# An adaLN transformer block on one core: weight loads, LN and modulation work reordered at the start, output transposes in two banks, and other slot counts

## Chip, cores and metric

The kernel runs on one core of a Trainium2 chip. Times are device microseconds of one execution; medians are over several executions. The profile is of one execution. A single-core program has no second die to compare with, so a run counts as slow only when it lies over 1.5% above the fastest of the same kernel.

## The reference

One block: a conditioning vector `c` gives six modulation vectors; then modulated layer norm (LN), attention over the last 512 cached keys and values (32 query heads, 4 KV heads), a gated residual, a second modulated LN, a SwiGLU FFN, and a gated residual.

```python
mod = (silu(c) @ w_mod).reshape(1, 6, 1, 1024)          # c: (1, 1024), w_mod: (1024, 6144)
sa, ca, ga, sb, cb, gb = (mod[:, i] for i in range(6))
h = layernorm(x) * (1 + ca) + sa                         # x: (1, 2048, 1024)
q = h @ wq                                               # 32 heads of 128
o = softmax(q @ k[-512:].T * 128**-0.5) @ v[-512:]       # per head; 8 query heads share a KV head
x = x + ga * (o @ wo)
h = layernorm(x) * (1 + cb) + sb
x = x + gb * ((silu(h @ w_gate) * (h @ w_up)) @ w_down)  # F = 3584
```

All inputs are bf16. The inputs, weights and matmuls are the same before and after.

## The kernel before

The tokens are processed in four chunks of 512. Everything is held transposed (features on partitions): `xT`, `hT`. A small recording layer (`T.op`) emits each instruction on its engine with the semaphore waits that its reads and writes of named buffers need. **Each engine, and the queue that issues the DMAs (SP), runs what it was given in program order** (moving one GpSimd instruction moved the squares behind it from 46.23 to 9.30 us, below), so where an operation stands in the program is a decision about what it waits behind.

The prologue, in program order (cuts marked with `...`):

```python
for t in range(4):                       # x tiles of chunk 0
    load_x_tile(t); transpose_x_tile(t)
for gi in range(4):                      # first third of w_mod, 3 slots of 1 MB
    load_wm(gi); mod_mm(gi)
mod_readout(0, 2 * DT, ...)              # shift and scale for the first LN
for t in range(4, 16):                   # the other x tiles, through 4 buffers
    load_x_tile(t); transpose_x_tile(t)
arena.reset()                            # K, V, wq slots overlap the w_mod slots
...
for gk in range(Hkv): T.op(Q_k, ... load K head gk ..., writes=[B_knat])   # one buffer record, one semaphore
for gk in range(Hkv): T.op(Q_v, ... load V head gk ..., writes=[B_vaug])
T.op(POOL, lambda: g.memset(v_aug[:, :, P:VW], 1.0), writes=[B_vaug])      # ones column of V
load_wq(0, 0); load_wq(0, 1)
... transpose K on TensorE ...
drain(ln1_task(0, OPB))                  # LN of chunk 0, whole: squares on POOL, sums on PE, ...
for ch in range(1, NCH): add_ln("ln1", ch, ln1_task(ch, OPB))   # background, a step at a time
```

All four K loads write one buffer record on one semaphore, so each waits for the landing of the one before it; the same for V. The memset waits for all V loads, and the LN's squares come after the memset on GpSimd (POOL).

The attention loop is software-pipelined: iteration `i` runs the query projection of head `i`, scores of `i-1`, PV of `i-2`, the output transpose of `i-3`, and one background step. In chunk 0 it also carries the rest of the modulation, 32 pieces:

```python
if i < 32:  load_wm_late(16 + i)                      # 128 columns of w_mod: rows of 256 bytes
if 2 <= i < 34:
    mod_mm_late(16 + i - 2)                           # 8 matmuls of one column into bank OA
...
qproj(i)                                              # 8 matmuls 128x512 into bank QB
if 0 <= i - 1 < NA: scores(i - 1)
if 0 <= i - 2 < NA: pv(i - 2)                         # into OA and OBT; VectorE scales out of OA (L573)
if 0 <= i - 3 < NA: otr(i - 3); ...
run_bg(1)
```

The modulation pieces share PSUM bank `OA` with PV. They stand first in an iteration, so they wait until VectorE has scaled the previous PV result out of that bank.

At the end of each FFN chunk the result is transposed back, all four tiles through one bank:

```python
for tt in range(TPC):
    for dt in range(DT): transpose(bb[...], xT[:, dt, ...], ..., PB[YTB])   # bank 6 every time
    T.op(DVE, lambda: V.tensor_copy(xnat[sl][:, :], bb[:, 0:D]), writes=[PB[YTB], B_xnat[sl]])
    T.op(Q_out[sl], ... store ...)
```

The softmax here doesn't subtract the row's maximum and nothing guards it: scores larger than these inputs give would overflow.

## Time and profile before

| | before |
|---|---|
| median of 16 runs | 1476.13 us (1475.0 to 1482.43) |
| span of the profiled run | 1473.2 us |
| TensorE busy / VectorE / ScalarE / GpSimd | 93% / 40% / 31% / 5% |
| first query projection ends | 70.25 us |

From the page of the kernel before: span, and two of the rows in 40 slices (busy tenths of TensorE, and granted TensorE clock in tenths of full speed).

```profile
span 1473.2 us, 20801 instructions
...
PE   4488889999999999999999999999999999989997
...
PEclk7599999999999999999999999999999999999999
```

TensorE is busy 90% or more in all slices but two from the seventh on (220 us), so time can mainly be won where it is not: at the start, and in gaps too short for such a row to show. The prologue, in the timeline of all engines (start us, duration us, engine, line, operation, out<-in, shapes, count, and in brackets the idle time before it and what ended it):

```profile
38.20 1.89 PE L288 MATMUL ps<-ident,arena 128*128 128x128 bf16 x16 [6.51 <-DMA arena<-in_A_k_cache_dram]
...
46.14 0.13 POOL L498 MEMSET arena<- 128x32 bf16 x1 [44.49 <-DMA arena<-in_A_v_cache_dram]
46.23 17.00 POOL L402 TENSOR_TENSOR ln_sq<-xT 128x512 bf16<-128x512 bf16 x16
...
54.31 0.61 PE L284 MATMUL ps<-ln_sq,ones_bf 128*128 128x512 bf16 x1 [0.39 <-POOL ln_sq L402]
55.03 0.69 DVE L415 SCALAR_TENSOR_TENSOR ln_var<-ps,ln_msq 128x512 f32<-128x512 f32 x1 [10.70 <-PE ps L284]
...
63.99 5.59 ACT L440 ACTIVATE hT<-ln_n,c6a,g 128x512 bf16<-128x512 bf16 x7 [0.82 <-DVE ln_n L437]
...
69.64 0.61 PE L284 MATMUL ps<-hT,arena 128*128 128x512 bf16 x1 [0.19 <-ACT hT L440]
```

The second line is the telling one: GpSimd had been idle for 44.49 us waiting for V, for a memset of 0.13 us, while x of chunk 0 had been in place since 9 us. The squares behind it, the variance behind them and the whole LN chain follow from there.

TensorE's timeline in chunk 0, and below the dots in chunk 1, where no modulation is left:

```profile
85.93 0.34 PE L284 MATMUL ps<-sc_bf,xnat 128*128 128x1 bf16 x8 [0.77 <-DVE arena L573]
86.13 1.89 PE L284 MATMUL ps<-hT,arena 128*128 128x512 bf16 x8
...
90.81 0.34 PE L284 MATMUL ps<-sc_bf,xnat 128*128 128x1 bf16 x8 [0.77 <-DVE arena L573]
...
330.39 1.89 PE L284 MATMUL ps<-hT,arena 128*128 128x512 bf16 x8
...
334.14 1.89 PE L284 MATMUL ps<-hT,arena 128*128 128x512 bf16 x8
```

An iteration takes 4.88 us (90.81 - 85.93) in chunk 0 and 3.75 us (334.14 - 330.39) in chunk 1. Of the 1.13 us between them, 0.20 us are the eight small matmuls themselves (86.13 - 85.93); 0.93 us is the wait, of which the profile names 0.77 us.

The output transposes of the second of the four chunks of the FFN, in TensorE's timeline:

```profile
1153.34 0.50 PE L288 MATMUL ps<-ident,xT 128*128 128x128 bf16 x6
...
1155.81 0.62 PE L288 MATMUL ps<-ident,xT 128*128 128x128 bf16 x8 [0.79 <-DVE xnat L729]
...
1158.62 1.04 PE L288 MATMUL ps<-ident,xT 128*128 128x128 bf16 x8 [0.79 <-DVE xnat L729]
1159.45 5.80 PE L284 MATMUL ps<-hT,arena 128*128 128x512 bf16 x21
```

Each tile waits 0.79 us for the copy out of the single bank. The trace's clock record has half clock granted from 1158.3 us for 3.4 us. Two groups from the list by form (busy us, mean ns, then idle before them and its releasers) sum the waits up:

```profile
L288 PE MATMUL ps<-ident,xT 128*128 128x128 bf16 x128 | 12.1, 232 | 12.3 <-DVE xnat L729 9.4 <-DVE xT L717 2.9
...
L284 PE MATMUL ps<-sc_bf,xnat 128*128 128x1 bf16 x256 | 10.9, 163 | 22.9 <-DVE arena L573 22.9
```

### The profile page before, as it was taken

To read this page: it belongs to the slowest core of one execution; us is meant where nothing else is said; L and a number is where in the kernel's file an instruction comes from. 1 tells how busy PE (TensorE), PEld (TensorE's weight loads), DVE (VectorE), ACT (ScalarE), POOL (GpSimd) and SP (SyncE) were. 2 spreads that over 40 slices of the span, in tenths; PEclk is the share of its full clock that TensorE was granted. 3 is DMA by queue.
4 is the path that set the end of the run, shared out by engine and by line. 5 is a ranking of instruction groups with operands and counts; after the bars stand their busy time and mean duration, and the time that the engine had idled before them with its cause. 6 is when DMAs were issued, how large, how long until landed. Compare 5 with 4: busy or idle time off the path is not lost.

```text
span 1473.2 us, 20801 instructions
## 1 busy us (share of the span) xinstructions
PE 1369.9 (93%) x8592; PEld 704.7 (48%) x8592; DVE 595.5 (40%) x1268; ACT 453.3 (31%) x722; POOL 68.7 (5%) x73
## 2 busy tenths in 40 slices
PE   4488889999999999999999999999999999989997
PEld 3144554456554556545564444444444444444443
DVE  3344554366561456515563144313431233123411
ACT  0255554266560466505673013201110011001100
POOL 0402001210001000010000100000000000000000
PEclk7599999999999999999999999999999999999999
DMA  7365440452214612046111774235633375328112
GB/s 239 103 165 137 108 108 30 115 161 74 74 39 114 172 58 87 30 114 172 59 58 31 227 228 144 100 101 193 222 115 100 123 234 171 94 92 270 59 51 79
DMA packets 262319, 178.55 MB, mean 121 GB/s; under 512 B 41040, under 2 KB 258128, under 8 KB 262224
## 3 DMA queue, kind: packets, MB, share of 16 engines
q1 hardware_dynamic: 262224, 177.22, 40.3%
q8 instruction: 67, 1.10, 0.3%
q14 instruction: 28, 0.23, 0.0%
HBM read 173.02 MB, written 4.19 MB: 120 GB/s over the span
## 4 chain that ended last, share of the span: by engine, by line
PE 89%; DVE 4%; DMA 2%; ACT 2%; issue 2%; POOL 0%; SPq 0%; DVEq 0%; ACTq 0%
PE ps L284 86%; PE ps L288 2%; DVE arena L573 1%; DMA arena<-in_w_mod_dram 1%; ACT arena L550 1%; DVE xT L717 1%; DMA arena<-in_A_v_cache_dram 1%; DVE xnat L729 1%; DMA arena<-in_A_k_cache_dram 1%; ACT hT L440 1%; POOL ln_sq L402 0%; DVE rl L570 0%; ACT L550 0%; ACT L422 0%; DMA xnat<-in_A_x_dram 0%
## 5 line engine op out<-in xcount | busy, mean ns | idle before, releaser
L284 PE MATMUL ps<-arena 128*128 128x512 bf16 (+1 forms) x4480 | 675.5, 307 | 14.8 <-DVE xT L717 11.0
L284 PE MATMUL ps<-hT,arena 128*128 128x512 bf16 x2816 | 635.9, 381 | 17.2 <-ACT hT L440 11.7
L284 PEld LDWEIGHTS ps<-arena 128*128 128x128 bf16 x4480 | 366.8, 98 | 339.2 <-issue 17.5
L284 PEld LDWEIGHTS ps<-hT,arena 128*128 128x128 bf16 x2816 | 269.4, 98 | 328.6 <-issue 11.9
L550 ACT ACTIVATE arena<-ps 128x512 bf16<-128x512 f32 x512 | 305.8, 597 | 295.0 <-PE ps L284 259.3
L697 ACT ACTIVATE arena<-ps 128x512 bf16<-128x512 f32 x112 | 66.9, 597 | 528.5 <-PE ps L284 528.5
L698 DVE SCALAR_TENSOR_TENSOR arena<-arena,ps 128x512 bf16<-128x512 bf16 x112 | 77.1, 688 | 175.9 <-ACT arena L697 175.9
L538 DVE CAST arena<-ps 128x512 bf16<-128x512 f32 x128 | 88.5, 691 | 85.1 <-PE ps L284 82.0
L402 POOL TENSOR_TENSOR ln_sq<-xT 128x512 bf16<-128x512 bf16 x64 | 67.8, 1081 | 734.7 <-PE ps L284 711.8
L701 DVE SCALAR_TENSOR_TENSOR arena<-arena,ps 128x512 bf16<-128x512 bf16 x112 | 77.1, 688 | 53.6 <-PE ps L284 53.5
L717 DVE SCALAR_TENSOR_TENSOR xT<-ps,c,xT 128x512 bf16<-128x512 f32 x32 | 22.6, 746 | 184.8 <-PE ps L284 184.8
L598 DVE SCALAR_TENSOR_TENSOR xT<-ps,c,xT 128x512 bf16<-128x512 f32 x32 | 24.0, 750 | 164.1 <-PE ps L284 164.1
L573 DVE TENSOR_TENSOR arena<-ps,rl 128x384 bf16<-128x384 f32 x128 | 71.4, 558 | 4.5 <-DVE rl L570 0.2
L569 DVE RECIPROCAL rl<-ps 128x3 f32<-128x3 f32 x128 | 23.1, 180 | 113.3 <-PE ps L284 113.3
L288 PE MATMUL ps<-ident,arena 128*128 128x128 bf16 x528 | 51.1, 221 | 7.9 <-DMA arena<-in_A_k_cache_dram 6.5
L584 DVE COPY arena<-ps 128x512 bf16<-128x512 bf16 x128 | 53.1, 415 | 0.2 <-PE ps L288 0.2
L575 DVE TENSOR_SCALAR arena<-ps,rl 128x128 bf16<-128x128 f32 x128 | 45.0, 351 | 4.6
L288 PEld LDWEIGHTS ps<-ident,arena 128*128 128x128 bf16 x528 | 35.6, 98 | 8.3 <-DMA arena<-in_A_k_cache_dram 6.7
L440 ACT ACTIVATE hT<-ln_n,c,g 128x512 bf16<-128x512 bf16 x32 | 25.8, 809 | 28.3 <-DVE ln_n L437 28.2
L440 ACT ACTIVATE hT<-ln_n,c6a,g 128x512 bf16<-128x512 bf16 x32 | 25.7, 811 | 23.2 <-DVE ln_n L437 23.2
L284 PE MATMUL ps<-sc_bf,xnat 128*128 128x1 bf16 x256 | 10.9, 163 | 22.9 <-DVE arena L573 22.9
L437 DVE TENSOR_TENSOR ln_n<-ln_t,ln_B 128x512 bf16<-128x512 bf16 x64 | 30.0, 469 | 1.3 <-DVE ln_t L434 0.2
(46 smaller groups left out, 246.1 us busy)
## 6 DMA issues: line engine op xcount, KB each, us to landing
arena<-in_A_wq_dram SPq DMA_DIRECT2D x32, 1024.0 KB, 5.4
arena<-in_A_wo_dram SPq DMA_DIRECT2D x16, 2048.0 KB, 9.8
arena<-in_B_w_gate_dram SPq DMA_DIRECT2D x28, 1024.0 KB, 5.2
arena<-in_B_w_up_dram SPq DMA_DIRECT2D x28, 1024.0 KB, 7.0
arena<-in_B_w_down_dram SPq DMA_DIRECT2D x16, 1792.0 KB, 10.1
xnat<-in_w_mod_dram SPq DMA_DIRECT2D x32, 256.0 KB, 3.1
xnat<-in_A_x_dram SPq DMA_DIRECT2D x16, 256.0 KB, 3.6
arena<-in_w_mod_dram SPq DMA_DIRECT2D x4, 1024.0 KB, 8.2
```

The lines of the kernel that those rows point to most:

```text
L284: T.op(PE, lambda: TE.matmul(out_ap, lhsT, rhs, start=start, stop=stop), reads=reads, writes=[bank_buf])
L288: T.op(PE, lambda: TE.transpose(out_ap, in_ap, ident[:, :]), reads=reads + [B_ident], writes=[bank_buf])
L402: T.op(POOL, lambda: g.tensor_tensor(ln_sq[dt][:, :], xT[:, dt, chs], xT[:, dt, chs], ALU.mult), reads=[B_xT[dt][ch]], writes=[B_sq[dt]])
L440: T.op(ACT, lambda: A.activation(hT[:, dt, chs], ln_n[sl][:, :], AF.Identity, bias=ccol[:, shift_base + dt:shift_base + dt + 1], scale=gco ...
L538: T.op(DVE, lambda: V.tensor_copy(qT_s[qs], bank(QB)), writes=[PB[QB], B_qT[qs]])
L550: T.op(ACT, lambda: A.activation(ex_s[es][:, kt, :], bank(b), AF.Exp, scale=att_scale), writes=[PB[b], B_ex[es]])
L573: T.op(DVE, lambda: V.tensor_tensor(o_s[os_][:, 0:3, :], in3, rl3, ALU.mult), reads=[B_rl], writes=[PB[OA], B_os[os_]])
L575: T.op(DVE, lambda: V.tensor_scalar(o_s[os_][:, 3, :], bank(OBT, P, 0), rl[:, 3:4], None, op0=ALU.mult), reads=[B_rl], writes=[PB[OBT], B_ ...
L584: T.op(DVE, lambda: V.tensor_copy(oT_all[:, h, :], bb[:, 0:CH]), writes=[PB[TRB], B_oT[h]])
L697: T.op(ACT, lambda: A.activation(th_s[ts_], bank(gb), AF.Tanh, scale=0.5), writes=[PB[gb], B_th[ts_]])
L698: T.op(DVE, lambda: V.scalar_tensor_tensor(out=t1_s[ts_], in0=th_s[ts_], scalar=1.0, in1=bank(gb), op0=ALU.add, op1=ALU.mult), reads=[B_th ...
L701: T.op(DVE, lambda: V.scalar_tensor_tensor(out=guT[:, ft, :], in0=t1_s[ts_], scalar=0.5, in1=bank(ub), op0=ALU.mult, op1=ALU.mult), reads= ...
```

## The change

Its intent: start the attention loop early, keep TensorE from waiting in chunk 0 and at the output, and give the FFN weights other slot counts. The core of the diff (renamings, asserts and the general sizing of the slots left out):

```diff
-            NWM = 3
+            NWM = 4
+            arena.off = ARENA_BYTES - NWM * DT * 512 * 2      # w_mod slots lie over oT_all, not over K, V, wq
...
+            ln0 = ln1_task(0, OPB, "act")                      # squares of chunk 0 on ScalarE
+            for _ in range(DT + 7):                            # statistics of LN 0 before the modulation
+                next(ln0)
             for gi in range(G1_READY + 1):
                 load_wm(gi)
                 mod_mm(gi)
             mod_readout(0, 2 * DT, c6a, B_c6a, 0, g1, B_g1, DT)
-            for t in range(TPC, ST):
-                load_x_tile(t)
-                transpose_x_tile(t)
...
-            Q_k = dq("q_k"); Q_v = dq("q_v")
+            Q_k = [dq("q_k%d" % i) for i in range(Hkv)]; Q_v = [dq("q_v%d" % i) for i in range(Hkv)]
...          # B_knat, B_vaug: one record per head as well
             load_wq(0, 0)
-            load_wq(0, 1)
+            drain(ln0)                                         # normalise, scale and shift: 8 activations
...
-            drain(ln1_task(0, OPB))
+            for t in range(TPC, 2 * TPC):
+                load_x_tile(t)
+            load_wq(0, 1)
...          # in the loop, i < 32:
-                    if i < NJ - JT0:
-                        load_wm_late(JT0 + i)
-                    if 2 <= i < NJ - JT0 + 2:
-                        mod_mm_late(JT0 + i - 2)
+                    if i == LATE_STEP * k: load_wm_late(gi)                  # 8 loads of 1 MB into unused hT, every 4th
+                    if TPC <= i < len(XT_REST): load_x_tile(XT_REST[i])
+                    if 1 <= i <= len(XT_REST): transpose_x_tile(XT_REST[i - 1])   # 12 x tiles, one each
                     qproj(i)
+                    if i == LATE_STEP * k + LATE_LEAD: mod_mm_late(gi)       # 32 matmuls, AFTER qproj
...
-                run_bg(1)
+                run_bg(2 if <an LN1 task is queued> else 1)
...          # last LN step of every chunk but the first: ScalarE activation -> VectorE tensor_scalar
...          # FFN
-            NWG = 3; NWD = 2
+            NWG = 2; NWD = 3
...
+                    yb = [6, 7][t % 2]                         # output transposes alternate banks
+                    bb = bank_bf(yb)
```

## The prediction

> **What bounds the kernel now.** From about 75 us on, TensorE. The timeline shows attention repeating every 3.75 us with no TensorE gap (chunk 1), FFN groups equally gapless, and matmuls 0.216 us apart. The chain of waits puts 89% on TensorE. That core of work is untouched. The time that can be won lies elsewhere:
>
> 1. *Prologue.* The first query projection ends at 70.2 us. Timeline: x tiles until 31 us, K loads one after another until 38 us, V loads until 46 us, and only then (GpSimd runs them behind the memset that waits for V) eight squares of 1.0 us until 54 us; then variance, Ln, a 1.28 us table load, Exp, and eight 0.81 us ScalarE activations.
> 2. *Late modulation in chunk 0.* Iterations take 4.88 us, not 3.75: 8 one-column matmuls (0.20 us) wait 0.77 us for VectorE's scaling that frees their bank. The group of sc_bf,xnat matmuls shows 22.9 us idle in front.
> 3. *Output transposes.* Per chunk three waits of 0.79 us for the copy out of the single bank: 9.4 us in all.
>
> **Prologue after.** The four w_mod loads, K, V and wq no longer wait for arena slots. LN of chunk 0 is taken before the modulation, squares on ScalarE. Estimate from the durations above: x transposed at 9 us, squares (0.8 us each, like the other bf16 activations) until 15.6, variance 17, Ln/table/Exp/B until 21; modulation matmuls 17 to 21, readout 22, then 8 x 0.81 us: first projection over near 30 us. Gain 40 us. The first matmuls stay slow: the Trainium skill (TensorE: Matmul & The Clock Gate, Part 1) says an idle array runs at half clock until about 3.4 us of activity; here spacing is 0.43 us until 75.7 us, then 0.21, and the granted clock between 40 and 80 us was 0.59.
>
> **Chunk 0 after.** 32 x 1.13 us goes. Back come 8 batches of 32 one-column matmuls (0.8 us each, 6.4 us; placed after the projection, when their bank has long been read); 12 x-tile transposes (8 x 0.057 us each, 5.5 us); some 4.5 us of stalls, since their copy (0.69 us) and twice the LN steps per iteration stand in VectorE's queue ahead of the score banks' release, and Ln, Exp and two table loads now meet in one iteration. Net gain 20 us.
>
> **FFN.** Two output banks: about 7.5 us of the 9.4. Gate/up double-buffered instead of triple: a 2 MB load lands in 7 us, needed after 13.8; with the 1.8 MB down-weights about 13 us of DMA per 13.8 us group: just enough, no gain. Activation moved to VectorE (0.3 to 0.7 us each, estimate): VectorE 40% busy, off the path; ScalarE's relief worth 1 us at most.
>
> Sum: 40 + 20 + 7.5 + 1 = 69: **1407 us, range 1394 to 1422**. Faster by over 2%: 0.97; within 2%: 0.03; slower: 0.00.
>
> **What would show it.** First query projection ending at 28 to 33 us; chunk 0 from there to its last output transpose about 151 us (171 before); no TensorE wait for the scaling before sc_bf matmuls; waits for the output copy under 2 us in all; chunks 1 to 3 and the gate/up stretches unchanged in length, no TensorE wait on gate or up weights.
>
> **What would make it wrong.** The weight loads sharing bandwidth so that the fourth w_mod or wq lands after 30 us; score banks stalling over 1 us in each of 12 iterations; gate/up weights late with two slots (several us per chunk); granted clock falling as density rises.

## The result, and the profile after

| | before | after |
|---|---|---|
| median | 1476.13 us (16 runs) | 1402.97 us (8 runs, 1400.38 to 1403.41) |
| ratio of fast runs | | 0.9495 (0.9483 to 0.9507) |
| span of the profiled run | 1473.2 us | 1399.8 us |
| mean granted clock | 0.979 | 0.995 |

Ratios here and below are the mean time of one kernel's fast runs over that of the other's of the same rounds, so not quite the ratio of the medians quoted.

The predicted 1407 us, range 1394 to 1422, held. Where the 73.4 us between the two profiled runs lie is read by cutting both at the same points of the program: the end of the first query projection, the first and the last read-out of attention's output projection, and the end. The busy time of each engine in each of these stretches, before and then after (start:end and length; busy us and instructions of TensorE, its weight loads, VectorE, ScalarE, GpSimd; granted clock, DMA share, GB/s):

```profile
0.00:70.25 70.25, 31.00 (x296) 18.46 (x296) 25.43 (x45) 11.81 (x14) 17.97 (x25) 0.68 0.59 180
70.25:249.10 178.85, 151.05 (x1369) 90.05 (x1370) 85.70 (x224) 92.20 (x149) 8.21 (x8) 0.98 0.43 113
249.10:846.80 597.70, 587.77 (x4097) 324.21 (x4096) 287.23 (x706) 272.59 (x435) 41.52 (x39) 1.00 0.35 98
846.80:1473.20 626.40, 600.08 (x2832) 272.00 (x2830) 197.09 (x294) 76.71 (x124) 1.04 (x1) 0.99 0.44 140
```

```profile
0.00:30.20 30.20, 16.66 (x202) 10.75 (x203) 14.37 (x33) 16.06 (x22) 1.02 (x9) 0.81 0.95 304
30.20:192.10 161.90, 154.25 (x1482) 95.96 (x1480) 100.77 (x252) 90.24 (x145) 24.45 (x24) 0.99 0.48 146
192.10:784.10 592.00, 582.78 (x4082) 322.21 (x4081) 295.58 (x738) 238.24 (x391) 32.91 (x31) 1.00 0.34 97
784.10:1399.80 615.70, 597.38 (x2832) 270.79 (x2830) 199.18 (x302) 70.70 (x116) 1.04 (x1) 1.00 0.45 144
```

Prologue 40.05 us less, chunk 0 16.95, the rest of attention 5.7, the FFN 10.7: together 73.4. The busy time of TensorE in the FFN barely moves; the length does.

The prologue after, in the timeline of all engines:

```profile
9.42 4.27 ACT L424 ACTIVATE ln_sq<-xT 128x512 bf16<-128x512 bf16 x8 [5.34 <-DVE xT L355]
...
15.13 2.54 PE L285 MATMUL ps<-sc_bf,arena 128*128 128x1 bf16 x96 [0.95 <-DVE ln_var L440]
...
20.57 0.51 SPq L539 DMA_DIRECT2D arena<-in_A_wq_dram  x1
...
21.38 6.38 ACT L466 ACTIVATE hT<-ln_n,c6a,g 128x512 bf16<-128x512 bf16 x8 [3.24 <-DVE ln_n L462]
...
26.61 3.59 PE L285 MATMUL ps<-hT,arena 128*128 128x512 bf16 x8 [5.27 <-DMA arena<-in_A_wq_dram]
```

The squares start at 9.42 us, as soon as x is there, and take 0.53 us each. The first projection is released by the landing of wq at 26.6 us; the last of the eight activations ends at 27.76 us (21.38 + 6.38). Two chains of nearly equal length meet here. In chunk 0 and at the output, from TensorE's timelines:

```profile
101.13 0.94 PE L285 MATMUL ps<-sc_bf,hT 128*128 128x1 bf16 x32
101.93 1.96 PE L285 MATMUL ps<-arena 128*128 128x512 bf16 x20
...
103.95 1.89 PE L285 MATMUL ps<-hT,arena 128*128 128x512 bf16 x8
...
107.70 1.89 PE L285 MATMUL ps<-hT,arena 128*128 128x512 bf16 x8
```

```profile
1088.42 0.50 PE L289 MATMUL ps<-ident,xT 128*128 128x128 bf16 x6
...
1090.88 1.22 PE L289 MATMUL ps<-ident,xT 128*128 128x128 bf16 x16 [0.34 <-DVE xnat L792]
1091.94 3.40 PE L285 MATMUL ps<-hT,arena 128*128 128x512 bf16 x15
```

The 32 modulation matmuls take 0.80 us with no wait, and an iteration without them takes 3.75 us already in chunk 0. The output transposes take 3.52 us (1091.94 - 1088.42) at full clock; before it was 6.11 us in the chunk shown and 5.74 us in the chunk ahead of it. The groups that answer to the two of before:

```profile
L289 PE MATMUL ps<-ident,xT 128*128 128x128 bf16 x128 | 10.5, 220 | 4.3 <-DVE xT L779 2.9 <-DVE xnat L792 1.4
...
L285 PE MATMUL ps<-sc_bf,hT 128*128 128x1 bf16 x256 | 7.5, 163 | 0.0
```

### The profile page after: what moved, and what is told of

Same layout as the page of the kernel before. It is cut to its first block, busy times and chain, and to the rows that moved or that the text cites. A ratio compares the mean times of both kernels' runs of the same rounds, so it can differ in the third digit from the quotient of the medians.

```text
span 1399.8 us, 20688 instructions
## 1 busy us (share of the span) xinstructions
PE 1351.1 (97%) x8592; PEld 699.7 (50%) x8592; DVE 609.9 (44%) x1324; ACT 415.2 (30%) x674; POOL 59.4 (4%) x65
## 4 chain that ended last, share of the span: by engine, by line
PE 93%; DVE 2%; ACT 2%; SPq 1%; issue 1%; DMA 0%; DVEq 0%; ACTq 0%
PE ps L285 90%; PE ps L289 3%; ACT arena L605 1%; DVE xT L779 1%; SPq L526 0%; SPq L361 0%; DMA arena<-in_A_wq_dram 0%; ACT L605 0%; ACT L447 0%; DVE xnat L792 0%; DVE arena L628 0%; SPq L530 0%; DVE ln_var L440 0%; ACT ln_var L447 0%; DVE arena L630 0%
## 5 line engine op out<-in xcount | busy, mean ns | idle before, releaser
L427 POOL TENSOR_TENSOR ln_sq<-xT 128x512 bf16<-128x512 bf16 x56 | 58.4, 1061 | 704.5 <-PE ps L285 681.1
L459 DVE TENSOR_TENSOR ln_t<-xT,ln_A 128x512 bf16<-128x512 bf16 x64 | 27.5, 430 | 0.0
L625 DVE RECIPROCAL rl<-ps 128x1 f32<-128x1 f32 x128 | 21.5, 168 | 13.6 <-PE ps L289 0.5
L285 PE MATMUL ps<-ln_sq,ones_bf 128*128 128x512 bf16 x64 | 15.1, 379 | 3.9 <-DVE arena L639 3.0
```

Of the source, the lines that this page charges most:

```text
L285: T.op(PE, lambda: TE.matmul(out_ap, lhsT, rhs, start=start, stop=stop), reads=reads, writes=[bank_buf])
L427: T.op(POOL, lambda: g.tensor_tensor(ln_sq[dt][:, :], xT[:, dt, chs], xT[:, dt, chs], ALU.mult), reads=[B_xT[dt][ch]], writes=[B_sq[dt]])
```

## The experiments

Twelve kernels. All outputs are right. The names beginning with b_ are the kernel before with one edit; those with a_ the changed kernel with one edit. They ran in three sessions, each beside its own runs of the kernel before (medians 1476.64, 1478.44 and 1476.17 us). To set an a_ kernel against the changed kernel, the text takes the difference of its ratio from 0.9495, times 1476 us; because the sessions differ, such a figure is good to about 3 us (each ratio's 95% interval is 2 to 4 us wide on either side). The trace gives the place.

| kernel | median us | ratio | against its parent | expected |
|---|---|---|---|---|
| b_mod_after_proj | 1451.63 | 0.9826 | -25.7 | -30 |
| b_two_out_banks | 1463.63 | 0.9909 | -13.4 | -8 to -10 |
| b_memset_later | 1472.44 | 0.9958 | -6.2 | -9 to -10 |
| a_mod_before_proj | 1407.12 | 0.9524 | +4.3 | +7 |
| a_one_out_bank | 1415.86 | 0.9578 | +12.3 | +9, or +11 to +17 |
| a_ln0_after_mod | 1411.94 | 0.9547 | +7.7 | +5 to +6 |
| a_wm_low | 1403.71 | 0.9494 | 0 | +5 to +8 |
| a_three_gate_slots | 1402.96 | 0.9484 | -1.6 | 0 |
| a_kv_one_by_one | 1412.44 | 0.9562 | +9.9 | +13 |
| a_x_before_loop | 1408.95 | 0.9540 | +6.6 | +2 to +5 |
| a_ln_on_scalar | 1404.45 | 0.9504 | +1.3 | 0 |
| a_four_banks_wq_first | 1386.14 | 0.9385 | -16.2 | -12 to -13 |

(The fourth column is the ratio's distance from 1, or from 0.9495, times 1476 us.)

### Chunk 0: position or batching?

The change both batches the late modulation (8 times 32 matmuls, from 1 MB loads, instead of 32 times 8 from loads of 256-byte rows) and moves it behind the projection. Two runs separate these.

```diff
 # b_mod_after_proj: kernel before
-                    if 2 <= i < NJ - JT0 + 2: mod_mm_late(...); ...
                     if h == 0: ensure_ln("ln1", ch)
                     qproj(i)
+                    if 2 <= i < NJ - JT0 + 2: mod_mm_late(...); ...
```

> Kernel before, with the 8 late modulation matmuls of each iteration emitted after the query projection instead of ahead of it; same 32 small loads of 256-byte rows, same 32 batches. Theory A (the wait for the bank on TensorE's path is the cost): iterations of chunk 0 fall from 4.88 us to 3.95 us, the 22.9 us of idle before the sc_bf,xnat matmuls fall below 2 us, and the time falls by about 30 us, to 1446 us (2.0% faster). Rival B (the many small loads or the number of batches are the cost, so that fewer and larger batches were needed): under 8 us, above 1468 us.

```diff
 # a_mod_before_proj: changed kernel
+                    for k, gi in ...: if i == LATE_STEP * k + LATE_LEAD: mod_mm_late(gi); ...
                     qproj(i)
-                    for k, gi in ...: if i == LATE_STEP * k + LATE_LEAD: mod_mm_late(gi); ...
```

> Changed kernel, with its 8 late modulation batches of 32 matmuls put back ahead of the query projection. Theory A (each batch ahead of the projection pays one bank wait of about 0.8 to 0.95 us, whatever its size): 8 x 0.9 = 7 us more than the changed kernel, 1410 us. Rival B (batching removed the cost, position does not matter): within 2 us of the changed kernel's 1403.

The kernel before with the move alone: iterations of 3.95 us (one small batch at 85.41 us, the next at 89.36), idle before the small matmuls 0.0 us instead of 22.9, and 25.7 us faster, with all 32 small loads and batches as they were. Theory A is borne out; the rival is not. Why less than 30? In the profiled runs chunk 0 became 24.5 us shorter: the wait had occurred 29 times, not 32 (29 x 0.93 = 27 us); the LN of chunk 1, at one step per shorter iteration, made TensorE wait 1.1 us more at the start of chunk 1; and half clock was granted there for 3.4 us (about 1.7 us). The rest of attention won 1.7 us and the FFN lost 4.3, in which there was more half clock; the next section has this.

The changed kernel with the batch put back ahead shows the same wait, once per batch, whatever the batch's size (0.77 us in five of the eight batches, 0.33 to 0.55 us in the three that fell among the x tiles). From TensorE's timeline of that kernel, where the same line was without a bracket in the changed one:

```profile
101.14 0.94 PE L285 MATMUL ps<-sc_bf,hT 128*128 128x1 bf16 x32 [0.77 <-DVE arena L628]
```

It cost 5.5 us between the profiled runs and 4.3 us timed, with 5.1 us of listed waits; 7 us was expected at 0.9 us for all eight. So position carries the gain. What batching adds is only that there would be 8 such waits instead of 32 if the position were bad.

### The output: waits, and something that follows them

```diff
 # b_two_out_banks: kernel before
-                bb = bank_bf(YTB)
+                    yb = [6, 7][t % 2]; bb = bank_bf(yb)       # per tile
```

> Kernel before, with the output transposes alternating between two PSUM banks, nothing else. Theory A (12 waits of 0.79 us for the copy, plus the last stretch of the kernel): 8 to 9 us less, 1467 to 1468 us. Theory B (the same, and a shorter gap also spares the half-clock stretch of 3.4 us seen at 1158 us, worth 1.7 us): about 10 us less, 1466 us, and no half clock in the FFN stretch. If the waits were not on the path: under 2 us less.

```diff
 # a_one_out_bank: changed kernel
-                    yb = [6, 7][t % 2]
+                    yb = 6
```

> Changed kernel, with the output transposes of all tiles back in one PSUM bank. Theory A (waits only): 12 waits of 0.79 us return less the 0.34 us waits of now, and the end of the kernel grows by 2 us: about 9 us more, 1412 us. Theory B (waits, and each longer stretch of transposes and waits, 5.7 us instead of 3.5 us without an ordinary matmul, is followed in some chunks by a stretch of granted half clock of 3.4 or 6.8 us, worth 1.7 or 3.4 us, where it falls being chance): 9 us and 2 to 8 us on top, 1414 to 1420 us, with half-clock records right at the output transposes; the unchanged gate/up matmuls after them run at half pace meanwhile.

Two banks alone took 13.4 us off the kernel before, and its FFN stretch became 615.9 us long, that of the changed kernel (615.7). One bank put back cost the changed kernel 12.3 us, and its FFN stretch became 627.9 us. Both are more than the waits: from 5.74 to 3.52 us is 2.2 us in each of three chunks, and the end of the kernel is 2.6 us shorter (from the first transpose that waits to the end, 8.55 and 5.99 us), 9.2 us in all. The rest follows theory B. The clock records of the profiled runs say where half clock was granted at the output transposes of the first three chunks:

| profiled run | banks | half clock at the three outputs (us granted) |
|---|---|---|
| before | 1 | 0, 3.4, 0 |
| b_mod_after_proj | 1 | 3.4, 3.4, 6.8 |
| b_memset_later | 1 | 3.4, 6.8, 6.8 |
| a_one_out_bank | 1 | 3.4, 0, 3.4 |
| b_two_out_banks, after, and 7 other a_ kernels with two banks | 2 | none, in 27 outputs |

9 of 12 outputs with one bank, none of 27 with two. The slow run, at a granted clock of 0.75 throughout, is left out. Half clock for 3.4 us costs a busy TensorE about 1.7 us, so by this estimate between 1.7 us (before) and 8.5 us (b_memset_later, 17 us of half clock) per run. Runs of the kernel before scatter accordingly: of two in one session, one took 1475.44 us at a mean granted clock of 0.979, the other 1481.08 us at 0.972 (over all 28 runs listed beside the experiments, time and clock correlate at -0.86).

The Trainium skill (TensorE: Matmul & The Clock Gate, Part 1) describes a free-running activity window of 3413 ns after which an idle array drops to half clock; the records agree: all but those that the end of the trace cuts last 3.413 us or a multiple, and in each fast trace every change of the clock lies on one grid of 3.413 us, to within 3 ns. Its Part 4 says that transposes do not count as busy in the same way. An estimate from that page's window: a stretch of 5.74 us without an ordinary matmul holds one whole window in about two of three cases ((5.74 - 3.41) / 3.41 = 0.68), one of 3.52 us in about 3%. The counts, 9 of 12 and 0 of 27, fit that, but the grid does not bear it out. In six of the 27 outputs with two banks a window covered 29 or 30 of the 32 transposes, with ordinary matmuls (all that are no transposes) busy in at most 6% of it, and full clock followed each time. So transposes in place of ordinary matmuls are not enough.

What differs with one bank is how long TensorE waits. Below is its busy time in four such windows (start:end and length; busy us and instructions; granted clock, DMA share, GB/s). The first three are of the kernel before: where the attention pipeline drains (half clock followed), the first output (full clock followed) and the second (half clock followed). The last is an output of the changed kernel (full clock followed):

```profile
786.22:789.63 3.41, 1.55 (x24) 1.00 0.00 0
1001.26:1004.67 3.41, 1.81 (x25) 1.00 0.40 154
1154.86:1158.27 3.41, 1.40 (x17) 1.00 0.26 102
...
1240.73:1244.14 3.41, 2.35 (x32) 1.00 0.03 13
```

With the grid laid over all 13 fast traces, 5036 windows after 90 us began at full clock. Where TensorE was busy for under 45% of one, half clock followed in 15 of 15; from 45% to 54.5%, in 11 of 19; above that, in none of 5002. This holds for the outputs (41% to 54% in the nine that were followed by half clock; 52% to 54% in the emptiest window of each of the other three with one bank; 69% in those six with two banks) and for the attention drain, which was followed by half clock in 7 of the 13 traces although ordinary matmuls stood less than 3.4 us apart there. So the waits thin out a window, and where the grid falls decides whether one window is thin enough. The two runs on the banks change only these waits; the rule itself is read off the traces, whose matmul ends are modelled, and no run tests its threshold.

### The prologue, piece by piece

```diff
 # b_memset_later: kernel before
-            T.op(POOL, lambda: g.memset(v_aug[:, :, P:VW], 1.0), writes=[B_vaug])
 ...
             drain(ln1_task(0, OPB))
+            T.op(POOL, lambda: g.memset(v_aug[:, :, P:VW], 1.0), writes=[B_vaug])
```

> Kernel before, with one GpSimd instruction (the memset of V's ones column) emitted after the squares of chunk 0 instead of ahead of them. Theory A (the squares stood behind a memset that waits for the last V load, though they need nothing of it): squares start at 9 us, the variance follows the K transposes at once, first query projection ends near 60 us instead of 70.2, time 9 to 10 us less, 1466 us. Rival B (the chain is set by the K and V loads themselves or by the order of TensorE's work): under 3 us less.

GpSimd's timeline of that kernel; the first line was at 46.23 us before:

```profile
9.30 8.02 POOL L402 TENSOR_TENSOR ln_sq<-xT 128x512 bf16<-128x512 bf16 x8 [7.65 <-DVE xT L351]
46.09 0.13 POOL L525 MEMSET arena<- 128x32 bf16 x1 [28.77 <-DMA arena<-in_A_v_cache_dram]
```

The first projection ended at 62.3 us instead of 70.25, so a 0.13 us memset on the wrong side of eight squares cost 8.0 us. Of that, the profiled run kept only 2.3 us in its span: its FFN stretch was 632.2 us instead of 626.4, with 17 us of half clock at the outputs. Here a gain at the start was given back by chance at the end. That is probably why only 6.2 us were timed, with runs from 1467.3 to 1473.7; the other runs have no trace.

```diff
 # a_kv_one_by_one: changed kernel
-            Q_k = [dq("q_k%d" % i) for i in range(Hkv)]; Q_v = ...
+            Q_k = [dq("q_k")] * Hkv; Q_v = [dq("q_v")] * Hkv       # and one buffer record for each
```

> Changed kernel, with one semaphore and one buffer record for all four K loads and one for all four V loads again, so each load waits for the landing of the one before. Theory A (this was the largest single piece of the prologue: in the kernel before, eight such loads took 15.5 us, 31.5 to 46 us with gaps, and wq stands behind them in the queue): K done near 28 us, V near 37, wq lands near 41, first projection ends near 44 us instead of 30.2, about 13 us more than the changed kernel, 1416 us. Rival (the place of the squares and the LN order made the gain): under 4 us more.

The K issues occupied the queue for 15.1 us and the V issues for 7.6 us; wq was issued at 33.0 us instead of 20.6, landed near 39.3, and the first projection ended at 42.9 us instead of 30.2. This is the largest single piece of the prologue that was found.

```diff
 # a_ln0_after_mod: changed kernel
-            for _ in range(DT + 7):
-                next(ln0)
```

> Changed kernel, with all of chunk 0's LN emitted after the modulation matmuls instead of its statistics ahead of them. My theory of the prologue as the trace now shows it (first projection bound by the landing of wq at 26.6 us, the LN chain only just behind with its last activation at 27.8 us): the squares still run at 9 us, but TensorE's sums wait for the fourth w_mod load, variance near 24 us, first activation near 29, first projection ends near 36 us instead of 30.2: 5 to 6 us more, 1409 us. Rival (LN chain has slack, the loads alone set the start): under 1.5 us more.

The first projection ended at 39.4 us, 9.2 later (7.7 us timed). The mechanism is the expected one, the size was not: TensorE was at half clock when it came to the first eight sums, 0.43 us each, so the variance came at 27.0 us and not 24, and the first activation at 32.4 us and not 29. The order matters although the squares still ran at 9 us.

```diff
 # a_wm_low: changed kernel
-            arena.off = ARENA_BYTES - NWM * DT * 512 * 2
```

> Changed kernel, with the four early w_mod slots at the start of the arena again, over the later K, V and wq slots. If the place in the arena matters: the first K load waits for the modulation matmuls of its slot, and wq for those of the last slot (near 19.5 us), so K lands after 22, wq after 32 us, the first projection ends at 35 to 38 us: 5 to 8 us more, 1408 to 1411 us. If not (the loads queue behind w_mod anyway): under 2 us more.

A miss: no loss in the timed runs, 2.7 us in the first projection's end (32.9 us), of which part is scatter: kernels untouched at this point ended it between 30.2 and 32.1 us. The K loads were indeed issued at 17.9 us instead of 10.2. But in the changed kernel the four K issues, begun at 10.23 us, hold the queue until 17.3 us; they stand behind 4 MB of w_mod in any case, the last of which landed at 18.5 us. The new place in the arena is worth little.

```diff
 # a_x_before_loop: changed kernel
-            XT_REST = list(range(TPC, ST))                     # one tile per iteration
+            for t in range(TPC, ST):                           # all ahead of the loop
+                if t >= 2 * TPC: load_x_tile(t)
+                transpose_x_tile(t)
+            XT_REST = []
```

> Changed kernel, with the other 12 x tiles loaded and transposed ahead of the loop (after the first LN and the K transposes) instead of one per iteration. Expected: first projection ends 9 to 12 us later (39 to 42 us); chunk 0 shorter by 12 x 0.46 us of transposes plus 1 to 3 us of stalls, 6 to 8 us; net 2 to 5 us more than the changed kernel, 1405 to 1408 us. If the in-loop copies and bank waits cost more than the model says (over 0.8 us an iteration), it is even or faster.

6.6 us slower, a little more than expected. Its profiled run was the one slow run (1796.68 us at a granted clock of 0.75); the other four lay between 1407.76 and 1411.16 us. Since only the slow run has a trace, the split between prologue and chunk 0 stays open. (Its first projection ended at 42.6 us, near the 39 to 42 expected, but at a granted clock of 0.5 to 0.75, so this is no more than a hint.)

### The parts that were predicted to do nothing

```diff
 # a_three_gate_slots: changed kernel
-            NWG = 2; NWD = 3        # and the loads one group ahead
+            NWG = 3; NWD = 2        # and the loads two groups ahead, as before
```

> Changed kernel, with three slots each for gate and up weights and two for down weights, and their load order, as before. Prediction's theory (both arrangements land in time, no TensorE wait on weights in either): within 1 us of 1403, no wait on gate, up or down loads. Rival (the new slots give part of the FFN gain of 10.7 us): 2 us or more slower.

```diff
 # a_ln_on_scalar: changed kernel
-                    if sq_eng == "act":
+                    if True:            # last LN step on ScalarE for every chunk
```

> Changed kernel, with the last LN step of every chunk on ScalarE again (0.81 us each there), all else as changed. Prediction's theory (neither engine bounds anything there): within 1.5 us of 1403. Rival (ScalarE's exps are delayed and TensorE waits for score banks): 2 us or more slower, with more TensorE idle put down to ScalarE.

Neither moved the time clear of the scatter (-1.6 and +1.3 us, with 3 us of uncertainty, and a 3.4 us half-clock stretch at the attention drain in each profiled run that the changed kernel's did not have). The traces are sharper: the FFN stretch took 615.7 us in both, as in the changed kernel, and TensorE waited for no gate, up or down weights in the changed kernel or in a_three_gate_slots. The LN step takes 0.81 us on ScalarE and 0.41 us on VectorE; nobody waits for it.

### Beyond both kernels

In the changed kernel, the largest wait of TensorE left is the same kind once more: the down projection's two accumulators, 11.0 us of listed idle. TensorE's timeline of the changed kernel:

```profile
910.33 0.38 PE L285 MATMUL ps<-arena 128*128 128x512 bf16 x1 [0.72 <-DVE xT L779]
910.90 12.04 PE L285 MATMUL ps<-arena 128*128 128x512 bf16 x55 [0.19 <-DVE xT L779]
923.66 0.38 PE L285 MATMUL ps<-arena 128*128 128x512 bf16 x1 [0.72 <-DVE xT L779]
```

```diff
 # a_four_banks_wq_first: changed kernel
-    DNB = [4, 5]
+    DNB = [[4, 5], [6, 7]]             # by pp % 2; output transposes use banks 4 and 5
 ...
+            load_wq(0, 0)              # ahead of the K and V loads instead of after them
```

> Beyond both kernels: the changed kernel with (1) the down projection's pairs of accumulators alternating between banks 4,5 and 6,7, the output transposes in 4,5, and (2) the first wq load issued ahead of K and V. From the changed kernel's waits: (1) 24 waits of TensorE on the down projection's read-out, 11.0 us, go; (2) first projection then bound by the last LN activation (27.8 us), so it ends at 28.2 to 29 us instead of 30.2, 1 to 2 us. Together 12 to 13 us, 1390 us. If bank waits of under 1 us were not wholly on the path, less than 6 us.

TensorE's timeline of that kernel, the whole down projection of a chunk:

```profile
882.70 48.51 PE L285 MATMUL ps<-arena 128*128 128x512 bf16 x220
931.05 0.50 PE L289 MATMUL ps<-ident,xT 128*128 128x128 bf16 x6
```

1386.14 us, 16.2 us less than the changed kernel and 6.2% less than before. The down projection takes 48.35 us (931.05 - 882.70) instead of 52.09 (884.02 to 936.11 in the changed kernel): 1.25 us per boundary, 15 us over twelve. The listed idle was 0.91 us per boundary. wq first brought only 0.6 us (first projection ends at 29.6 us): now each matmul waits for an LN activation, 0.8 us apart, and these came later than in the changed kernel, as the modulation matmuls did (16.6 instead of 15.1 us).

## Why the prediction was right

- **TensorE bounds the kernel, and its work is untouched.** Right. Its busy time in the FFN fell by under 3 us of 600; a gate/up stretch of 448 matmuls takes 96.86 us before and after, and 97.97 us only where half clock fell on it (from 1159.45 us, before).
- **Prologue, 40 us.** Right in size: 40.05 us, the first projection ends at 30.2 us (28 to 33 predicted). The path there was only half right. The squares took 0.53 us on ScalarE and not 0.8, so the last activation came at 27.8 us, and the landing of wq at 26.6 us became the releaser; the prediction had named only a landing after 30 us, as a risk. The pieces: K and V loads one after another (12.7 us), the order of LN and modulation (9.2 us), the memset (8.0 us in the kernel before). They are measured in two different kernels and overlap, so they do not add up to 40. The arena slots, which the prediction named first, were worth nothing clear. Not tested alone: the squares on ScalarE instead of GpSimd (0.53 us each, and 1.0 us on GpSimd), the fourth w_mod slot, and in a fast trace the 12 x tiles ahead of the loop.
- **Chunk 0, net 20 us.** 16.95 us between the same points. By the prediction's own measure, from the first projection to the last output transpose, chunk 0 took 155.0 us (185.17 - 30.21) and not 151. The difference is bookkeeping for the most part: with two LN steps per iteration, the statistics of chunk 2 now run before the output projection, not in it, and bring 6.35 us with them (16 matmuls, 3.46 us, and waits of 1.40 and 1.49 us). Without these it is 23.3 us. The 4.5 us allowed for stalls by the x tiles was too much: the trace shows three waits at the x tiles, of 0.82, 0.78 and 0.25 us. Against that, 29 waits went and not 32; and about 1.9 us, by estimate, came from something that the prediction did not count: 2.2 us of half clock at the start of this stretch instead of 6.0.
- **No TensorE wait for the scaling.** Right: 22.9 us to 0.0, and the position alone does it.
- **The rest of attention unchanged.** It is 5.7 us shorter: 3.46 us are the statistics matmuls that moved out of it, and 1.7 us a half-clock stretch at 789.6 us that the profiled run of the changed kernel does not have.
- **FFN, 7.5 us and no gain from the slots.** 10.7 us. The waits gave 9.2, and 1.5 us more is the half-clock stretch that followed the long output. This is the one mechanism that the prediction lacked; it had feared the opposite (clock falling as density rises). The skill's half clock after idleness was cited for the start only, and the same trace showed it at 1158 us.
- **Slots and the engine of the last LN step: nothing.** Right, within scatter.

The sum, 69 us, came out 4 us short of 73 because the FFN term was 3.2 us too small and the rest of attention was given nothing, against 3 us too much in chunk 0 and 1 us for ScalarE's relief that no run shows. That these partly cancel is luck.

## What to carry to other kernels

On an engine that executes in order, a small instruction that waits for something far away holds up everything behind it: look for a tiny operation with a huge idle time in front of it (here 0.13 us behind 44.49), and for loads tied to one semaphore without need. A wait of TensorE for a PSUM bank to be read out is paid in full and a bit more than the profile lists (0.93 for 0.77 us, 1.25 for two waits of 0.91 together: 0.16 to 0.17 us per wait, which is how much longer than their spacing of 0.216 us the last matmul before it is recorded, 0.38 us), so measure such a cost by the period of the loop, and remove it by another position or another bank. Short gaps that follow each other can also bring half clock on what comes after (here where they left TensorE busy for about half of a 3.4 us window or less), at random from run to run, so judge such an edit by several runs and by the clock record.

## What the Trainium skill lacked or had wrong

- TensorE: Matmul & The Clock Gate, "Why this matters for your kernels", advises no idle gaps over about 3 us. That row alone would pass the output with one bank, where no listed gap exceeded 0.79 us, and half clock still followed 9 of 12; TensorE was busy for 41% to 54% of the 3.413 us window before it.
- The same page's Part 4 says that full clock does not engage for transposes, which do not count as busy in the same way. Here six windows with 29 or 30 transposes and almost no ordinary matmul, TensorE busy for 69% of each, were followed by full clock, and the transposes in them stood 0.056 us apart.
- ScalarE: Activation LUTs, "What ACT_TABLE_LOAD costs", gives 1283 ns for the load and 2.66 us for a switch with its drain. The trace has 1.28 us for the load, but Ln ended at 16.20 us, the load ran from 16.22 to 17.50 and Exp began at 17.52: a switch of 1.32 us.
